# A gated mix of sliding-window attention and a SwiGLU block on one core: transposed scores that skip a place, another deal of product steps, later early tiles, and V's first quarter ordered by kind

## The chip, the cores and the metric

The kernel runs on one core of a Trainium2 chip. The metric is the device time of one execution in microseconds, and the runs of a kernel are summarised by their median. All times in this document are microseconds unless ns is written.

## The reference, cut to what matters

```python
def reference(A_x, A_wqkv, A_wo, B_x, B_w_gate, B_w_up, B_w_down, gate_w):
    x = A_x                                          # 1 x 2048 x 512
    g = _sigmoid((x * gate_w).sum(-1, keepdims=True))
    a = _A_ref(x, A_wqkv, A_wo)      # 32 heads of 16, window of 256 keys
    b = _B_ref(x, B_w_gate, B_w_up, B_w_down)   # silu(x wg) * (x wu), times wd; F = 1792
    return g * a + (1 - g) * b
```

The attention is causal within a window: query i sees keys i - 255 to i. Scores are scaled by 1/4, go through a softmax, weigh the values, and the heads are projected by `wo`. All is float32.

## The kernel before

Products that must be exact to float32 are made of three products of rounded halves: each operand is split into a rounded part (`hi`, or names that end in h) and the remainder (`lo`, or names that end in l), and hi x hi, hi x lo and lo x hi are summed in a bank of PSUM. There are eight banks, kept under the names pa, pb, pc and pd, two each, which are dealt out in turn by `bank`. The order of work on every engine is written out by hand: what stands first in the program is issued first on its queue.

**Prologue (lines 119 to 272).** x and the weights of V come by DMA in four blocks k of 128 rows of the contraction. Each block is split, the rounded part on ScalarE (ACT), the remainder on VectorE (DVE) for x and, for V's weights, on DVE for block 0 and on GpSimd (POOL) for blocks 1 to 3 (lines 173 to 178). V's first quarter (four blocks b of rows of x, in four accumulators, two to each of pa and pb) is summed k by k as the blocks come, and within a k block by block: for each b its three products (lines 214 to 217). The rest of V and the products of Q and K follow (line 381).

**The attention stage (lines 469 to 843).** Heads go in eight groups g of four. Time is counted in slots k; four slots make a step t, and sixteen steps a group. In each slot, one score of a coming group is made (`stage1`, a matmul at line 603, then a masked maximum on DVE at line 605) and one transposed score (`stage2`, a matmul at line 642, then the exponential on ACT at line 644, then selections on POOL at lines 646 and 649). Scores and transposed scores use 64 or 63 rows of the array, and each belongs to one half of the rows; two matmuls on different halves run at once. The remaining time is filled with steps of `stream`, the gate and up products of the SwiGLU block (line 564): in a step each half of the rows does one product of 512 columns, and a sum over 12 products per half is copied out by ACT (`copy_out`, line 511) in the slot where its second half ends. How many steps a slot gets is `DEAL[t >= g7][part][hd]`, with `part` the step's place among four and `hd` the slot in the step; g7 = 112 is the first step of the last group.

Every fourth step t (part 0, from t = 4 on), after the steps of slot 1, a value product is issued (`av`, line 664): 96 matmuls of 64 rows by 32 columns, each in two passes, or 64 of them where a group begins, into one bank of pc and one of pd, which `evacuate` then copies out: ACT the second bank (line 675), DVE the first (line 681; in the last group line 677 adds the two). Below, a visit is a value product with the slots up to the next. In this stage pd has two banks; transposed scores take them in turn, and the value product takes one in between. From t = 112 on, there are no scores left; transposed scores are issued two at a time in slots 0 and 2, out of three banks.

**The last group** also prepares what the next stage needs. `tile_early` makes the first two tiles of silu(gate) x up: an exponential on ACT (line 748), four operations on DVE (lines 749 to 752, the reciprocal at 750 the longest), and the split into halves, ACT first and then DVE (line 753). Each operation is hung on a slot through `at` (lines 787 to 790); the tile's inputs are loaded at slots 4 (g7 + 9) + 1 and + 2 (line 786). `prepare` splits the next weights of the stream (ACT a cast, POOL the remainder), three slots after the last sum of the ones before. After the last step, tile 2 goes through the Silu of ACT (line 760), which needs another table.

**The final stage (from line 845)** multiplies the tiles by `wd`, projects the attention's output and writes the result.

Of the kernel before, what the change touches and what calls it, by code (L numbers as in the profile page):

```python
# [12 lines left out]
ALU = mybir.AluOpType  # L13
# [5 lines left out]
NK = D // P  # L19
NB = S // P  # L20
CH = 512
NCH = S // CH
G = H // 4
NF = F // P
VW = 4 * (DH + 1) + DH
NSLOT = 4
# [7 lines left out]
def gated_mix(ctx, tc, xT, xn, wqk, wv, wo, wgu, wd, gw, out):  # L34
# [4 lines left out]
    nc = tc.nc  # L39
# [27 lines left out]
    def split(hi, lo, src, hi_eng, lo_eng):  # L67
        if hi_eng is nc.scalar:
            nc.scalar.copy(hi, src)
        else:  # L70
            hi_eng.tensor_copy(hi, src)
        lo_eng.tensor_tensor(out=lo, in0=src, in1=hi.bitcast(F32), op=ALU.subtract)
# [14 lines left out]
    def run(gen, n=None):  # L87

        while n is None or n > 0:
            if next(gen, run) is run:  # L90
                break
            n = n and n - 1
# [19 lines left out]
    def bank(n):  # L112
        names = BANKS[n if isinstance(n, str) else ("pa", "pb", "pc", "pd")[n]]
        names.append(names.pop(0))
        return psum.tile([P, CH], F32, name=names[-1])
# [7 lines left out]
    wvh = vpool.tile([P, NK, D], F32R, name="wvh")  # L123
    wvl = vpool.tile([P, NK, D], F32R, name="wvl")
# [8 lines left out]
    def u_tile():  # L133
        return wide.tile([P, CH], F32, name="u", bufs=6)
# [6 lines left out]
    def xk(c, k):  # L141
        return halves_of(xraw[2 * c + k // 2])[k % 2]

    wvraw = [u_tile() for _ in range(NK)]
# [20 lines left out]
    def fill_v(t):  # L165
        nc.gpsimd.memset(t, 0.0)
        for i in range(2):
            nc.gpsimd.memset(t[:, :, i, :68].rearrange("p g (j e) -> p g j e", e=17)[:, :, :, DH], 1.0)

    def split_x(c, k):  # L170
        split(xhi[c][:, k], xlo[c][:, k], xk(c, k), nc.scalar, nc.vector)

    for k in range(NK):
        split_x(0, k)
        split(wvh[:, k], wvl[:, k], wvraw[k], nc.scalar, nc.vector if k == 0 else nc.gpsimd)
        if k == 1:
            fill_v(vs[0])
    fill_v(vs[1])

    def v_products(b):  # L180
        c, o = divmod(b * P, CH)
        return [(xt[c][:, k, o:o + P], wt[:, k]) for k in range(NK)
                for xt, wt in ((xhi, wvh), (xhi, wvl), (xlo, wvh))]
# [24 lines left out]
    def vproj(b, ps, ks=range(NK)):  # L208
        todo = v_products(b)
        for k in ks:  # L210
            for n in range(3 * k, 3 * k + 3):
                nc.tensor.matmul(ps, *todo[n], start=n == 0, stop=n == 3 * NK - 1)

    first = [bank(n // 2) for n in range(4)]
    for k in range(NK):
        for b in range(4):
            vproj(b, first[b], (k,))
    for c in (1, 2):
# [250 lines left out]
    with ExitStack() as A:  # L469
# [14 lines left out]
        def at(k, *fs):  # L484
            AT.setdefault(k, []).extend(fs)
# [14 lines left out]
        def tick_end():  # L500
            for f in AT.pop(NOW[0], ()):
                f()
# [88 lines left out]
        def stage1(g, qb):  # L591

            hf, b = divmod(qb, NB // 2)
            if b == 0:
                MX[g, hf] = sm.tile([P, 4, NB // 2], F32, name="mx")
            q0, k0 = qb * P, max(0, qb - 2) * P
            n = q0 + P - k0
            for hd in range(4):
                pr, j = divmod(hd, 2)
                r = slice(64 * j, 64 * j + 63)  # L600

                ps = bank("pd") if g == 0 and pr else bank("pc")
                nc.tensor.matmul(ps[:, :n], QT[g % 2][pr][r, q0:q0 + P], KT[g % 2][pr][r, k0:k0 + n],  # L603
                                 start=True, stop=True)
                mx = nc.vector.tensor_tensor_reduce(out=ps[:, :n], in0=ps[:, :n], in1=mask[:, 3 * P - n:],  # L605
                                                    scale=1.0, scalar=NEG, op0=ALU.add, op1=ALU.max,
                                                    accum_out=MX[g, hf][:, hd, b:b + 1])
                if g == 0:
                    BEHIND.append(mx)
                yield  # L610
# [20 lines left out]
        def stage2(g, kb):  # L631


            n = min(3, NB - kb) * P
            k0 = kb * P
            for hd in (1, 0, 3, 2):
                pr, j = divmod(hd, 2)
                r = slice(64 * j, 64 * j + 64)
                if j:
                    pt = PT[g, kb, pr] = ptp.tile([P, 2, 3 * P], F32, name="pt")  # L640
                ps = bank("pd")
                nc.tensor.matmul(ps[:, :n], KT[g % 2][pr][r, k0:k0 + P], QT[g % 2][pr][r, k0:k0 + n],  # L642
                                 start=True, stop=True)
                BEHIND.append(nc.scalar.activation(pt[:, j, :n], ps[:, :n], AF.Exp, scale=SCALE))  # L644
                if not j:
                    nc.gpsimd.affine_select(out=pt[:, :, :P], in_=pt[:, :, :P], pattern=[[0, 2], [1, P]],  # L646
                                            compare_op=ALU.is_ge, fill=0.0, base=0, channel_multiplier=-1)
                    if n == 3 * P:
                        nc.gpsimd.affine_select(out=pt[:, :, 2 * P:], in_=pt[:, :, 2 * P:],  # L649
                                                pattern=[[0, 2], [-1, P]], compare_op=ALU.is_ge, fill=0.0,  # L650
                                                base=-1, channel_multiplier=1)
                yield
# [34 lines left out]
        first = chain(*(stage1(0, b) for b in range(NB)))  # L687
# [52 lines left out]
        def tile_load(n, place):  # L740
            GOT[n] = [h.bitcast(F32) for h in halves_of(pieces[place])]
            for i in range(2):
                nc.sync.dma_start(GOT[n][i], raws[n, i, 0])

        def tile_early(n):
            gt, up = GOT[n]
            sg, TILE[n] = kept(), halves_of(pieces[TILE_AT[n]])
            for f in (lambda: nc.scalar.activation(sg, gt, AF.Exp, scale=-1.0),
                      lambda: nc.vector.tensor_scalar(sg, sg, 1.0, None, op0=ALU.add),
                      lambda: nc.vector.reciprocal(sg, sg),  # L750
                      lambda: nc.vector.tensor_tensor(out=sg, in0=gt, in1=sg, op=ALU.mult),
                      lambda: nc.vector.tensor_tensor(out=sg, in0=up, in1=sg, op=ALU.mult),
                      lambda: split(*TILE[n], sg, nc.scalar, nc.vector)):
                f()
                yield
# [28 lines left out]
            wd_early(4 * (g7 + 1 + m) + 2, m, m)  # L784
        for n in range(2):
            at(4 * (g7 + 9) + 1 + n, lambda n=n: tile_load(n, RAW_AT[n]))
        for n, ticks in enumerate(((1, 3, 3, 3, 3, 12), (7, 9, 9, 9, 9, 19))):
            early = tile_early(n)
            for m in ticks:
                at(4 * (g7 + 10) + m, lambda early=early: run(early, 1))  # L790
# [11 lines left out]
            spread(4 * (16 * g + 9) + 3, 1, stack(g + 2, 0))  # L802
            spread(4 * (16 * g + 17) + 1, 1, stack(g + 2, 1))

        DEAL = [[[(hd + 1) * n // 4 - hd * n // 4 for hd in range(4)] for n in deal] for deal in ((5, 9, 8, 8), (8, 8, 8, 8))]
        DEAL[0][0] = 1, 2, 2, 0
        scores = chain(*(stage1(*divmod(b, NB)) for b in range(NB, G * NB)))
        run(scores, 1)
        for t in range(G * NB + 1):
            g, i = divmod(t, NB)  # L810
            d, part = divmod(t, NSLOT)
            s2 = stage2(g, i) if t < G * NB else iter(())
            values = part == 0 and t > 0
            if t == g7:
                BANKS["pc"].remove("pb1")
                BANKS["pd"].append("pb1")
            for hd in range(4):
                k = NOW[0] = NSLOT * t + hd
                run(scores, 1)
                if t < g7:  # L820
                    run(s2, 1)
                elif hd % 2 == 0:
                    run(s2, 2)
                if t == G * NB and hd == 0:
                    last_tile = tile_silu(2)
                    run(last_tile, 1)
                if t < G * NB:
                    run(steps, DEAL[t >= g7][part][hd])
                if hd == 1 and values:
                    av(*divmod(d - 1, NCH))  # L830
                    for f in LULL.pop(k, []) + UNDER:
                        f()
                    UNDER.clear()
                    evacuate(*divmod(d - 1, NCH))
                tick_end()
            if i in (7, 15) and g + 1 < G:
                UNDER.append(lambda g=g, i=i: put_max(g + 1, i // 8))
            if t >= 10 and t % 4 == 2 and t + 6 < G * NB:
                load_v((t + 6) // 4)
# [195 lines left out]
```

## Time and profile before

| | us |
|---|---|
| median of three runs (822.34 to 822.65) | 822.5 |
| the profiled execution | 822.11 |
| its span, first to last instruction | 820.4 |
| outside the span | 1.7 |

A row of a timeline reads: start, length, engine, line, operation, output <- inputs, shape, count, and in brackets the engine's idle time before it and what ended that. PE is TensorE's matmuls, PEld its weight loads, POOL GpSimd, q an engine's queue. Lengths of matmuls are modelled and overlap, so starts tell more than lengths. A row of the stages (two numbers with a colon) reads: from and to, width, busy time of PE, PEld, DVE, ACT and POOL with the count of instructions, TensorE's granted clock, the share of the DMA engines and GB/s. The granted clock is 1.00 in every row used here.

### The profile page before, as it was taken

The page shows a single profiled execution, that of the slowest core. Times are in us where ns is not written, and L with a number is a line of the kernel's source. Part 1 is how long each engine was busy: PE and PEld are TensorE (multiplying, and loading weights), DVE is VectorE, ACT ScalarE, POOL GpSimd, SP SyncE. Part 2 cuts the span into 40 slices and gives each one's busy share as a digit, 9 for nine tenths or more (in the row PEclk, how much of TensorE's full clock was granted, in tenths as well). Part 3 has the DMA queues.
Part 4 walks back from the last instruction along what each step waited for, and adds up shares of the span by engine and source line. Part 5 has one row for each costly group of instructions (what it writes and reads, how often), then busy time and mean ns, then how long its engine had stood idle before and what let it go on. Part 6 is the DMA issues. An engine that isn't in the chain of part 4 may idle for free.

```text
span 820.4 us, 20498 instructions
## 1 busy us (share of the span) xinstructions
PE 812.0 (99%) x7681; PEld 681.0 (83%) x7681; DVE 550.4 (67%) x1425; ACT 470.0 (57%) x956; POOL 402.1 (49%) x715
## 2 busy tenths in 40 slices
PE   9999999999999999999999999999999999999997
PEld 7888888878888888888888888888887888888886
DVE  5675554248877888878888887786576666554652
ACT  7455553312576767767677676776776563435340
POOL 5124442260366666767667576665873205442320
PEclk9999999999999999999999999999999999999999
DMA  8446666385625654566555655352659997878611
GB/s 302 148 156 254 231 231 235 137 268 178 218 85 194 189 179 157 182 213 202 171 167 168 207 188 159 132 170 89 212 191 349 271 287 229 273 226 221 213 52 52
DMA packets 80211, 159.70 MB, mean 195 GB/s; under 512 B 14960, under 2 KB 19440, under 8 KB 80112
## 3 DMA queue, kind: packets, MB, share of 16 engines
q1 hardware_dynamic: 68544, 127.44, 47.5%
q0 software_dynamic: 10992, 29.91, 11.3%
q8 instruction: 60, 0.98, 0.5%
q10 hardware_dynamic: 576, 1.05, 0.4%
q14 instruction: 39, 0.32, 0.1%
HBM read 93.32 MB, written 65.01 MB: 193 GB/s over the span
## 4 chain that ended last, share of the span: by engine, by line
PE 95%; DMA 2%; DVE 1%; ACT 1%; POOL 0%; SPq 0%; issue 0%; DVEq 0%; ACTq 0%
PE pa L564 22%; PE pb L564 10%; PE pd L642 6%; PE pc L664 5%; PE pd L381 4%; PE pb L381 4%; PE pa L381 4%; PE pd L81 3%; PE pc L81 3%; PE pc L83 3%; PE pd L83 3%; PE pc L82 3%; PE pd L82 3%; PE pb L664 2%; PE pc L381 2%; PE pb L83 2%
## 5 line engine op out<-in xcount | busy, mean ns | idle before, releaser
L644 ACT ACTIVATE pt<-pd 128x384 f32<-128x384 f32 (+2 forms) x491 | 223.0, 474 | 43.9 <-PE pd L642 25.6
L605 DVE CUSTOM_DVE_ANT_0 pc<-pc,mask 128x384 f32<-128x384 f32 (+2 forms) x322 | 173.2, 548 | 23.5 <-PE pc L603 9.6
L642 PE MATMUL pd<-q,k 64*128 64x384 f32 (+2 forms) x491 | 167.2, 348 | 1.8 <-ACT pt L644 1.8
L564 PE MATMUL pa<-xhi,wh 64*128 64x512 f32 x492 | 168.5, 395 | 0.0
L564 PE MATMUL pa<-xlo,wh 64*128 64x512 f32 x492 | 167.6, 394 | 0.0
L564 PE MATMUL pa<-xhi,wl 64*128 64x512 f32 x492 | 165.9, 395 | 0.0
L646 POOL TENSOR_SCALAR_AFFINE_SELECT pt<-pt 128x256 f32<-128x256 f32 x256 | 110.9, 434 | 67.9 <-ACT pt L644 62.7
L642 PEld LDWEIGHTS pd<-q,k 64*128 64x128 f32 x491 | 90.8, 185 | 26.1 <-ACT pt L644 9.8
L603 PE MATMUL pc<-k,q 63*128 63x384 f32 (+2 forms) x322 | 106.9, 337 | 0.0
L564 PE MATMUL pb<-xhi,wl 64*128 64x512 f32 x244 | 96.2, 394 | 0.0
L564 PE MATMUL pb<-xhi,wh 64*128 64x512 f32 x244 | 96.2, 394 | 0.0
L564 PE MATMUL pb<-xlo,wh 64*128 64x512 f32 x244 | 96.2, 394 | 0.0
L649 POOL TENSOR_SCALAR_AFFINE_SELECT pt<-pt 128x256 f32<-128x256 f32 x224 | 94.3, 421 | 0.0
L605 DVE CUSTOM_DVE_ANT_0 pb<-pb,mask 128x384 f32<-128x384 f32 (+2 forms) x158 | 86.9, 550 | 6.9 <-PE pb L603 3.0
L564 PEld LDWEIGHTS pa<-xhi,wh 64*128 64x128 f32 x492 | 88.2, 185 | 1.9 <-DVE mx L605 0.5
L564 PEld LDWEIGHTS pa<-xhi,wl 64*128 64x128 f32 x492 | 87.0, 185 | 1.1
L564 PEld LDWEIGHTS pa<-xlo,wh 64*128 64x128 f32 x492 | 86.9, 185 | 0.6
L605 DVE DVE_READ_ACCUMULATOR2_ANT mx<- 128x1 f32 x512 | 72.8, 142 | 0.0
L921 DVE TENSOR_TENSOR sg<-got,sg 128x512 f32<-128x512 f32 x52 | 41.1, 790 | 45.2 <-ACT sg L920 39.4
L664 PE MATMUL pd<-pt,vg 64*32 64x320 f32 (+4 forms) x1184 | 63.1, 346 | 0.0
L603 PEld LDWEIGHTS pc<-k,q 63*128 63x128 f32 x322 | 58.6, 184 | 4.8 <-issue 4.3
L682 POOL TENSOR_TENSOR oe<-oe,ob 128x512 f32<-128x512 f32 (+1 forms) x28 | 35.2, 1256 | 54.5 <-ACT ob L675 51.5
(307 smaller groups left out, 2050.8 us busy)
## 6 DMA issues: line engine op xcount, KB each, us to landing
got<-raws SPq DMA_DIRECT2D x104, 256.0 KB
raws<-ev SPq DMA_DIRECT2D x91, 256.0 KB
q<-xd SPq DMA_DIRECT2D x96, 128.0 KB
k<-xd SPq DMA_DIRECT2D x96, 128.0 KB
xd<-cx SPq DMA_DIRECT2D x16, 512.0 KB
xd<-cy SPq DMA_DIRECT2D x16, 512.0 KB
od<-oe POOLq DMA_DIRECT2D x32, 256.0 KB, 3.4
raw<-wgu SPq DMA_DIRECT2D x25, 256.0 KB
```

The source lines that it names most:

```text
L81: nc.tensor.matmul(ps, lh, rh, start=start and i == 0, stop=False, skip_group_check=skip)
L82: nc.tensor.matmul(ps, lh, rl, start=False, stop=False, skip_group_check=skip)
L83: nc.tensor.matmul(ps, ll, rh, start=False, stop=stop and i == n - 1, skip_group_check=skip)
L381: nc.tensor.matmul(ps, l[:, w], r[:, k], start=n in (1, 2, 5) and k == m == 0, stop=k == 1 and m == 2, skip_group_check=True)
L564: mm = nc.tensor.matmul(ps[o], w[r], x[r], start=first and i == 0, stop=(o is odd or bool(lane)) and i == turn - 1)
L603: nc.tensor.matmul(ps[:, :n], QT[g % 2][pr][r, q0:q0 + P], KT[g % 2][pr][r, k0:k0 + n], start=True, stop=True)
L605: mx = nc.vector.tensor_tensor_reduce(out=ps[:, :n], in0=ps[:, :n], in1=mask[:, 3 * P - n:], scale=1.0, scalar=NEG, op0=ALU.add, op1=ALU.m ...
L642: nc.tensor.matmul(ps[:, :n], KT[g % 2][pr][r, k0:k0 + P], QT[g % 2][pr][r, k0:k0 + n], start=True, stop=True)
L644: BEHIND.append(nc.scalar.activation(pt[:, j, :n], ps[:, :n], AF.Exp, scale=SCALE))
L646: nc.gpsimd.affine_select(out=pt[:, :, :P], in_=pt[:, :, :P], pattern=[[0, 2], [1, P]], compare_op=ALU.is_ge, fill=0.0, base=0, channel_mu ...
L649: nc.gpsimd.affine_select(out=pt[:, :, 2 * P:], in_=pt[:, :, 2 * P:], pattern=[[0, 2], [-1, P]], compare_op=ALU.is_ge, fill=0.0, base=-1, ...
L664: nc.tensor.matmul(AV[g, c][h][32 * j:32 * j + 32, q0 - c * CH:q1 - c * CH], VG[4 * g + kb // 4][o, kb % 4, 17 * j:17 * j + 32], PT[g, kb, ...
```

## The change

Four edits. In the prologue, block 0 of V's weights is rounded by DVE rather than ACT, ahead of the splits of x on DVE's queue; and the first quarter's products of k = 0 are issued by kind, the four blocks' hi x hi first, then the four with the weights' remainder, then the four with x's remainder. In the attention stage, the transposed scores become one chain over all steps: in slot 2 of every step with a value product none is issued, so that the chain runs one place late, and in slot 1 of part 2 two are issued, which catches up. The deal of steps for t < 112 becomes 6, 8, 8, 8 over the four parts in place of 5, 9, 8, 8, with part 0 as 1, 2, 2, 1. In the last group, tile 0's exponential moves one slot later and tile 1's split three slots later.

```diff
+    nc.vector.tensor_copy(wvh[:, 0], wvraw[0])
+    nc.vector.tensor_tensor(out=wvl[:, 0], in0=wvraw[0], in1=wvh[:, 0], op=ALU.subtract)
     for k in range(NK):
         split_x(0, k)
-        split(wvh[:, k], wvl[:, k], wvraw[k], nc.scalar, nc.vector if k == 0 else nc.gpsimd)
+        if k:
+            split(wvh[:, k], wvl[:, k], wvraw[k], nc.scalar, nc.gpsimd)
         if k == 1:
             fill_v(vs[0])
...
     first = [bank(n // 2) for n in range(4)]
-    for k in range(NK):
+    for n in range(3):
+        for b in range(4):
+            nc.tensor.matmul(first[b], *v_products(b)[n], start=n == 0, stop=False)
+    for k in range(1, NK):
         for b in range(4):
             vproj(b, first[b], (k,))
...
-        for n, ticks in enumerate(((1, 3, 3, 3, 3, 12), (7, 9, 9, 9, 9, 19))):
+        for n, ticks in enumerate(((2, 3, 3, 3, 3, 12), (7, 9, 9, 9, 9, 22))):
...
-        DEAL = [[[(hd + 1) * n // 4 - hd * n // 4 for hd in range(4)] for n in deal] for deal in ((5, 9, 8, 8), (8, 8, 8, 8))]
-        DEAL[0][0] = 1, 2, 2, 0
+        DEAL = [[[(hd + 1) * n // 4 - hd * n // 4 for hd in range(4)] for n in deal] for deal in ((6, 8, 8, 8), (8, 8, 8, 8))]
+        DEAL[0][0] = 1, 2, 2, 1
         scores = chain(*(stage1(*divmod(b, NB)) for b in range(NB, G * NB)))
+        transposed = chain(*(stage2(*divmod(b, NB)) for b in range(G * NB)))
...
-            s2 = stage2(g, i) if t < G * NB else iter(())
...
                 if t < g7:
-                    run(s2, 1)
-                elif hd % 2 == 0:
-                    run(s2, 2)
+                    run(transposed, 0 if t and (part, hd) == (0, 2) else 2 if t > NSLOT and (part, hd) == (2, 1) else 1)
+                elif t < G * NB and hd % 2 == 0:
+                    run(transposed, 2)
```

## The prediction

> **What bounds the kernel now.** The page's head and its chain come first, then the stages.
>
> ```profile
> span 820.4 us, 20498 instructions
> ...
> PE 95%; DMA 2%; DVE 1%; ACT 1%; POOL 0%; SPq 0%; issue 0%; DVEq 0%; ACTq 0%
> 226.37:568.38 342.01, 342.01 (x4854) 290.47 (x4851) 277.66 (x950) 245.05 (x545) 228.10 (x476) 1.00 0.52 168
> ```
>
> TensorE sets the end, so the change can only give time where TensorE stands or starts late. The last row (width, then busy time of PE, PEld, DVE, ACT, POOL) is the stage with value products up to the last group. Its busy PE hides stalls, since matmuls are pipelined and two run at once on the two halves of the rows. I therefore read starts. An undisturbed slot first:
>
> ```profile
> 348.32 0.34 PE L603 MATMUL pc<-k,q 63*128 63x384 f32 x1
> 348.50 0.34 PE L642 MATMUL pd<-q,k 64*128 64x384 f32 x1
> ...
> 348.97 0.34 PE L603 MATMUL pb<-k,q 63*128 63x384 f32 x1
> ```
>
> A slot with two scores and two product steps takes 0.65 here (348.32 to 348.97), and a score holds its half 0.18. Behind a value product:
>
> ```profile
> 343.99 0.34 PE L642 MATMUL pd<-q,k 64*128 64x384 f32 x1
> ...
> 344.18 0.39 PE L564 MATMUL pa<-xhi,wh 64*128 64x512 f32 x1
> 344.29 0.34 PE L603 MATMUL pc<-k,q 63*128 63x384 f32 x1
> 344.41 0.39 PE L564 MATMUL pa<-xlo,wh 64*128 64x512 f32 x1
> 344.54 0.44 PE L642 MATMUL pd<-q,k 64*128 64x384 f32 x1
> 344.65 0.40 PE L603 MATMUL pb<-k,q 63*128 63x384 f32 x1
> 344.93 0.44 PE L642 MATMUL pd<-q,k 64*128 64x384 f32 x1
> ...
> 345.50 0.33 PE L603 MATMUL pc<-k,q 63*128 63x384 f32 x1
> ...
> 346.13 0.34 PE L603 MATMUL pc<-k,q 63*128 63x384 f32 x1
> ```
>
> A product holds its half 0.23 (344.18 to 344.41). The half of the score at 344.29 has that score, one transposed score and two products before its next score at 345.50: 2 x 0.18 + 2 x 0.23 = 0.82, but 1.21 pass, 0.39 too many. The other half, from 344.65 to 346.13, holds two scores and four products: 1.28, and 1.48 pass, 0.20 too many. The mean, **0.30 lost behind a value product**, is what the first edit is about. Who is waited for (total, times, longest), and ACT there:
>
> ```profile
> PEld pd L642 <- ACT pt L644: 5.6, 28, 0.4
> PEld pd L642 <- ACT ob L675: 5.2, 26, 0.2
> ```
>
> ```profile
> 343.90 0.59 ACT L675 COPY ob<-pd 128x512 f32<-128x512 f32 x1 [1.99 <-POOL wl L72]
> 344.38 0.50 ACT L644 ACTIVATE pt<-pd 128x384 f32<-128x384 f32 x1
> ```
>
> Transposed scores have two pd banks and the value product takes one. So the score at 344.54 waits for the bank that ACT copies out from 343.90, and that at 344.93 for the exponential from 344.38 to 344.88, itself behind the copy.
>
> **The scores that skip a place.** With nothing in slot 2, the first transposed score comes in slot 3 in the free bank, the next in slot 4 in the copied one, about 0.15 after the copy is out (344.49, wanted near 344.7). The third wants the first's bank two slots on. Both waits go: 27 visits (t = 4 to 108) x 0.30 = **8.1 gained**. ACT then idles until slot 3's score; its later work covers that no more than now.
>
> Three visits have a cast of weights in that place as well:
>
> ```profile
> 281.11 0.62 ACT L69 CAST wh<-raw 128x512 fp32r<-128x512 f32 x1
> ```
>
> ```profile
> 281.85 0.33 PE L603 MATMUL pb<-k,q 63*128 63x384 f32 x1
> 282.17 0.44 PE L642 MATMUL pd<-q,k 64*128 64x384 f32 x1
> ...
> 283.37 0.34 PE L603 MATMUL pc<-k,q 63*128 63x384 f32 x1
> ```
>
> The score at 282.17 is 0.14 late (281.85 + 0.18 is 282.03). Up to its next score at 283.37 this half holds two scores and four products, 1.28, but 1.52 pass: 0.24 in all, 0.10 of it behind the wait, in the restart. With the skip the cast runs before the first exponential: 3 x 0.24 = **0.7 gained**.
>
> What it adds: at part 2, slot 1, two transposed scores stand in one slot, and the second wants the bank of the score one slot earlier on its own half: 0.18 + 2 x 0.23 + 0.18 = 0.82 later. A bank's turn (score, exponential, release) is 0.94 (343.99 to 344.93). So a **new wait** of 0.12, and behind it in PE's queue stand that slot's four products. It costs between nothing (if the other half, whose own transposed score is issued ahead of it, and the loads behind it absorb it) and 0.22 (wait plus restart as at 282.17). I take 0.10, as the other half is busy through most of it: 27 x 0.10 = **2.7 lost**.
>
> **The deal.** The count of steps stays 30 a visit, and a sum ends every 12. Counted from the loops, sums that ended in slots 4, 9, 15 of even visits now end in 3, 9, 15; 7, 12 of odd ones become 6, 12. Each end puts a copy on ACT, which holds it 0.48 (as the copy of the same shape at 343.90 does, up to 344.38). In the 13 even visits it falls between the first and the second late exponential. That one is then some 0.68 late (the two late scores come some 0.25 apart and an exponential runs 0.50, so 0.20 behind the first, then 0.48 behind the copy), and the bank's slack is 2 x 0.65 - 0.94 = 0.36: a wait of 0.32. Bounds: nothing, or 0.32 + 0.10 = 0.42; the nearest row is the cast above, of a like length between two exponentials, so 0.24: **3.1 lost**. In the 14 odd visits it lies two slots ahead of the double score and may delay its bank by up to half the copy; between 0 and 0.24 I take 0.10, near the lower end because two slots of ACT's slack lie between: **1.4 lost**. Sum of both edits: 8.8 - 7.2 = 1.6 gained. POOL's selections (228.10 busy of 342.01) and DVE (277.66) follow with room; the last scores before a value product keep their slots, so its inputs are no later.
>
> **The early tiles.** No DMA moves with them. Tile 0:
>
> ```profile
> 600.96 0.63 ACT L748 ACTIVATE ev<-k 128x512 f32<-128x512 f32 x1 [0.45 <-DMA k<-raws]
> 601.49 0.60 ACT L69 CAST wh<-raw 128x512 fp32r<-128x512 f32 x1
> ```
>
> ```profile
> 601.22 0.33 PE L642 MATMUL pb<-q,k 64*128 64x384 f32 x1
> 602.53 0.44 PE L642 MATMUL pd<-q,k 64*128 64x384 f32 x1 [0.99 <-ACT pt L644]
> ```
>
> ACT waits 0.45 for the tile's load, then runs its exponential (0.53 to the cast) before the scores' exponentials that TensorE needs. One slot later, those start 0.45 + 0.53 = 0.98 sooner, and the tile's exponential delays the next pair by up to 0.53. Between 0.45 and 0.98 I take 0.7; DVE's work on the tile hangs on the same exponential and starts 0.6 or so later, with its reciprocal off the path. Tile 1's halves:
>
> ```profile
> 615.33 0.62 ACT L69 CAST q<-ev 128x512 fp32r<-128x512 f32 x1 [1.01 <-DVE ev L752]
> ...
> 618.85 0.63 ACT L760 ACTIVATE ev<-k 128x512 f32<-128x512 f32 x1
> ```
>
> ```profile
> 615.35 0.22 PE L642 MATMUL pb<-q,k 64*128 64x128 f32 x1
> 616.18 0.32 PE L642 MATMUL pd<-q,k 64*128 64x128 f32 x1 [0.61 <-ACT pt L644]
> ```
>
> ACT stands 1.01 for DVE with the last exponentials behind it, and TensorE 0.83. Three slots later they go first. What is late next is ACT's own chain: cast, copy, table load and Silu run until 619.48 now, and the copy that frees the last value product's bank is queued behind them, so part of the 0.83 comes back there. Between 0 and 0.83 I take 0.4. Both: **1.1 gained**.
>
> **V's first quarter.**
>
> ```profile
> 10.73 1.55 POOL L72 TENSOR_TENSOR wvl<-u,wvh 128x512 fp32r<-128x512 f32 x1
> ```
>
> ```profile
> 6.72 0.62 ACT L69 CAST xhi<-q 128x512 fp32r<-128x512 f32 x1 [0.45 <-DMA q<-xT]
> ```
>
> ```profile
> L71 DVE CAST k<-ev 128x512 fp32r<-128x512 f32 x4 | 2.4, 607 | 1.0 <-DMA ev<-wd 1.0
> ```
>
> ```profile
> 7.06 0.50 PE L212 MATMUL pa<-wvl,xhi 128*128 128x512 f32 x1 [0.23 <-DVE wvl L72]
> ...
> 12.64 0.39 PE L212 MATMUL pa<-wvl,xhi 128*128 128x512 f32 x1
> ```
>
> By kind, four products run on the first weights before their remainder is needed, so the 0.23 of idling before 7.06 goes. DVE's copy (607 ns where it makes the same cast elsewhere) replaces one on ACT of 0.62, so the first weights come no later; ACT's next cast is no sooner for it, since it waits for x (6.72, idle 0.45 before). From the third block on the remainder that POOL ends at 12.28 (10.73 + 1.55) binds: its product can start near 12.33, not 12.64. So **0.3 gained**, which is also the upper bound while POOL binds; the lower is 0.
>
> **Sum.** 1.6 + 1.1 + 0.3 = 3.0 off the profiled 822.11 (its span 820.4 and 1.7 around it) is 819.1. The runs' median is 0.39 above that execution, so I forecast **819.5**.
>
> **Rivals.** *Waits absorbed:* TensorE's queue swallows the new waits; 8.8 + 1.4 = 10.2 gained, 812.3. For it: L642 waits for pt only 28 times in the stage's 342 us; against it: the 0.94 turn. 0.10.
>
> *Halves start in order:* then the double score would hold the other half's products too, 0.18 on one half, 0.09 in the mean, 27 x 0.09 = 2.4 more: 821.9, no change.
>
> ```profile
> 180.54 0.39 PE L564 MATMUL pb<-xhi,wh 64*128 64x512 f32 x1
> 180.55 0.44 PE L603 MATMUL pc<-k,q 63*128 63x384 f32 x1
> 180.78 0.39 PE L564 MATMUL pb<-xlo,wh 64*128 64x512 f32 x1
> ```
>
> Here the loop issues three products of one half before the scores, yet a score on the other half starts ahead of the second product. So 0.07. The Trainium skill ("TensorE: Matmul & The Clock Gate", Part 3, The mechanism) says that matmuls start and end strictly in program order and only weight loads are pulled ahead; by that the sum would be this rival's, and this trace disagrees (180.55 before 180.78).
>
> *The stall only moves:* new waits eat all 8.8 and the last group gives nothing but the prologue: 822.2; 0.11.
>
> *ACT binds (slower):* every new wait costs its upper bound, 27 x 0.22 + 13 x 0.42 + 14 x 0.24 = 14.8 against 8.8; with 1.4 from the rest 4.6 lost: 827.1. It decides from a mean price of 0.38 a visit on. For it: the 0.94 turn and the cast's 0.24; against: ACT is busy 245.05 of 342.01. 0.27.
>
> **How the numbers follow.** Forecast 0.45 (own range 816.5 to 820.8), absorbed 0.10, in order 0.07, moved 0.11, ACT binds 0.27, which starts at 824.2. A measurement tells 0.2%, 1.6, from no change. Faster 0.55, same 0.18, slower 0.27. The range 815.3 to 826.0 leaves out most of the first rival and the upper end of the last.
>
> **What would show it.** Right: behind value products no transposed score waits for ob, L642's waits for pt move to part 2 slot 1, and the stands of 1.31 and 0.83 in the last group shrink; TensorE's 12.64 row comes near 12.33. Wrong: waits of 0.3 and more in slots 6 and 9 of every visit.

## The result and the profile after

| | before | after |
|---|---|---|
| median of the timed runs | 822.42 us (822.07 to 822.75) | 825.67 us (825.46 to 826.73) |
| the profiled execution | 822.11, span 820.4 | 825.46, span 823.7 |

The changed kernel takes 1.0035 of the time of the one before (95% interval 1.0019 to 1.005): 3.3 us slower, where 819.5 was forecast. The time lies in the range, the sign is wrong.

The first fence is the changed kernel's page: its head and its chain by engine. The second is its view by windows for the same stage as before, from t = 4, the step of the first value product, to the first step of the last group.

```profile
span 823.7 us, 20498 instructions
...
PE 98%; DMA 1%; DVE 0%; ACT 0%; POOL 0%; issue 0%; DVEq 0%; ACTq 0%
```

```profile
core 0: us, PE busy (x) PEld busy (x) DVE busy (x) ACT busy (x) POOL busy (x), PEclk, DMA share, GB/s
226.25:571.76 345.51, 345.47 (x4855) 293.09 (x4851) 273.44 (x950) 243.46 (x545) 229.54 (x476) 1.00 0.52 167
```

The stage took 342.01 and now takes 345.51: the whole loss, 3.50, is in the visits. ACT and DVE are no busier there (243.46 and 273.44 after, 245.05 and 277.66 before), POOL by 1.4, and the clock stays full. So the loss is a wait. The view of waits for this stage says whose (total, times, longest):

```profile
PEld pd L648 <- ACT pt L650: 12.9, 60, 0.3
```

The changed file has six more lines ahead of this place, so L648 is the transposed score that was L642, L650 its exponential. The 26 waits for the copied bank (ob) are gone, as the edit meant. The waits for an exponential rose from 28 to 60, and their sum from 5.6 to 12.9. In the visit that the prediction quoted, the transposed scores behind the value product now start without a stand. The first three of them in the timeline of TensorE:

```profile
345.65 0.33 PE L648 MATMUL pd<-q,k 64*128 64x384 f32 x1
...
345.87 0.36 PE L648 MATMUL pd<-q,k 64*128 64x384 f32 x1
...
346.71 0.34 PE L648 MATMUL pd<-q,k 64*128 64x384 f32 x1
```

These take their lengths of 0.33 to 0.36; the two that waited were 0.44 long before, which is how a restart shows. Four slots on comes the place with two transposed scores, slot 9 of an even visit. TensorE there, and below it its weight loads:

```profile
348.84 0.33 PE L648 MATMUL pd<-q,k 64*128 64x384 f32 x1
...
349.30 0.35 PE L648 MATMUL pd<-q,k 64*128 64x384 f32 x1
349.48 0.34 PE L609 MATMUL pc<-k,q 63*128 63x384 f32 x1
349.75 0.44 PE L648 MATMUL pd<-q,k 64*128 64x384 f32 x1
349.76 0.67 PE L570 MATMUL pa<-xlo,wh 64*128 64x512 f32 x2
350.09 0.57 PE L570 MATMUL pa<-xhi,wl 64*128 64x512 f32 x2
350.33 0.34 PE L609 MATMUL pb<-k,q 63*128 63x384 f32 x1
350.50 0.50 PE L570 MATMUL pa<-xhi,wh 64*128 64x512 f32 x1
```

```profile
349.20 0.18 PEld L648 LDWEIGHTS pd<-q,k 64*128 64x128 f32 x1
349.25 0.18 PEld L609 LDWEIGHTS pc<-k,q 63*128 63x128 f32 x1
349.75 0.18 PEld L648 LDWEIGHTS pd<-q,k 64*128 64x128 f32 x1 [0.32 <-ACT pt L650]
349.75 0.29 PEld L570 LDWEIGHTS pa<-xlo,wh 64*128 64x128 f32 x2
```

The second score of the pair (349.75) wants the bank of the score at 348.84, 0.91 earlier: the bank's turn, as foreseen. What was not foreseen is what stands with it. The wait is on the score's weight load, and no load behind it in the queue starts before it, for either half: the other half's product load comes at 349.75 too. That other half had ended its score at 349.30 + 0.18 = 349.48, starts its product at 349.76 (0.28 lost), and its next score at 350.33, where two products of 0.23 would have ended at 350.22 (0.11, the restart): 0.39. The waiting half loses 0.09 (349.66 to 349.75) and 0.11 (349.75 + 0.18 + 0.46 is 350.39, the next product 350.50): 0.20. The mean is 0.30, to the hundredth what a value product's wait cost before (0.39 and 0.20). In all 27 visits, no product of slot 9 starts on either half before the second score of the pair.

In odd visits the bank's turn itself is longer. There a sum ends in slot 6, and ACT's copy of it (361.32) stands ahead of the exponentials of slots 7 and 8. ACT in the next visit, which is odd, then the transposed score of slot 8 and the weight load of the second score of the pair, which wants its bank:

```profile
361.32 0.59 ACT L517 COPY ev<-pa 128x512 f32<-128x512 f32 x1
361.80 0.88 ACT L650 ACTIVATE pt<-pd 128x384 f32<-128x384 f32 x2
```

```profile
361.63 0.33 PE L648 MATMUL pd<-q,k 64*128 64x384 f32 x1
```

```profile
362.73 0.18 PEld L648 LDWEIGHTS pd<-q,k 64*128 64x128 f32 x1 [0.20 <-ACT pt L650]
```

The turn is 1.10 here; by the starts in the trace it is 1.05 to 1.16 in odd visits, and 0.91 in all even ones but one (1.04). So in odd visits the loss in slot 9 is that of the pair and of the copy together, and no run here parts them.

The sum of the time lost, made as above for every slot of the 27 visits (how far each half's queue has come at its end, less 0.175 for each score and 0.228 for each product, which is how undisturbed ones follow each other, mean of both halves), gives the table below; it is worked out from all starts in the trace. Slot 2, with the value product itself, is left out.

```text
lost per visit, us, in slot     3    4    5    6    7    8    9   10   11   12   13   14   15
before, even visits           .05  .31  .02  .01  .07  .01  .00  .00  .00  .08  .01  .00  .00
after, even visits            .00  .04  .01  .21  .01  .01  .31  .11  .01  .01  .01  .00  .00
before, odd visits            .04  .29  .07  .01  .00  .00  .00  .00  .00  .01  .02  .02  .07
after, odd visits             .01  .04  .02  .01  .02  .01  .35  .01  .01  .02  .02  .03  .08
```

In the last group, the chain of waits of the changed kernel runs as follows (start, length, what). Below it stand the last value product in TensorE's timeline and POOL's timeline ahead of it:

```profile
618.62 0.83 DVE k L72
619.45 0.94 DVE den L464
620.38 0.28 issue
620.67 0.50 POOL rd L466
621.23 0.43 POOL raws L518
621.66 0.12 issue
621.78 0.43 POOL pt L652
622.25 0.32 PE pc L670 x8
```

```profile
618.57 2.22 PE L670 MATMUL pc<-pt,vg 64*32 64x320 f32 x66
622.25 0.88 PE L670 MATMUL pc<-pt,vg 64*32 64x64 f32 x30 [1.47 <-POOL pt L652]
```

```profile
620.67 0.56 POOL L466 DMA_DIRECT2D rd<-den  x1 [0.90 <-DVE den L464]
621.23 0.55 POOL L518 DMA_DIRECT2D raws<-ev  x1
621.78 0.77 POOL L652 TENSOR_SCALAR_AFFINE_SELECT pt<-pt 128x256 f32<-128x256 f32 x2
```

Both stands of 0.99 and 0.61 that the early tiles caused have shrunk, and the last value product now waits 1.47 in their stead. POOL's queue holds a DMA (rd<-den) that waits for DVE's reciprocal of the denominators (L464), and the last selections stand behind that DMA. Before, they stood so too. TensorE and POOL there:

```profile
616.84 2.68 PE L664 MATMUL pc<-pt,vg 64*32 64x320 f32 x96
```

```profile
617.06 0.56 POOL L460 DMA_DIRECT2D rd<-den  x1 [0.53 <-DVE den L458]
617.62 0.55 POOL L512 DMA_DIRECT2D raws<-ev  x1
618.17 0.77 POOL L646 TENSOR_SCALAR_AFFINE_SELECT pt<-pt 128x256 f32<-128x256 f32 x2
```

Counted from the first step of the last group (568.38 before, 571.76 after), the last selections start at 49.79 before and at 50.02 after, 0.2 later, and so does the reciprocal they stand behind (47.43 and 47.67). The value product starts at 48.46 before and at 46.81 after, 1.65 sooner. So the 1.47 is for the most part TensorE coming sooner to selections that came just in time before and have not moved with it.

### The profile page after: what moved, and what is told of

It reads as the page before. It is cut to its first block, busy times and chain, and to the rows that moved or that the text cites. A ratio compares the mean times of both kernels' runs of the same rounds, so it can differ in the third digit from the quotient of the medians.

```text
span 823.7 us, 20498 instructions
## 1 busy us (share of the span) xinstructions
PE 815.5 (99%) x7681; PEld 683.0 (83%) x7681; DVE 550.0 (67%) x1426; ACT 467.9 (57%) x955; POOL 404.3 (49%) x715
## 3 DMA queue, kind: packets, MB, share of 16 engines
q10 hardware_dynamic: 576, 1.05, 0.4%
## 4 chain that ended last, share of the span: by engine, by line
PE 98%; DMA 1%; DVE 0%; ACT 0%; POOL 0%; issue 0%; DVEq 0%; ACTq 0%
PE pa L570 23%; PE pb L570 11%; PE pd L648 6%; PE pc L670 5%; PE pd L387 4%; PE pb L387 4%; PE pa L387 4%; PE pd L81 3%; PE pc L81 3%; PE pc L83 3%; PE pd L83 3%; PE pc L82 3%; PE pd L82 3%; PE pc L609 2%; PE pb L670 2%; PE pc L387 2%
## 5 line engine op out<-in xcount | busy, mean ns | idle before, releaser
L650 ACT ACTIVATE pt<-pd 128x384 f32<-128x384 f32 (+2 forms) x491 | 219.3, 475 | 49.2 <-PE pd L648 26.3
L648 PE MATMUL pd<-q,k 64*128 64x384 f32 (+2 forms) x491 | 164.7, 348 | 0.3 <-ACT pt L650 0.2
L570 PE MATMUL pa<-xhi,wl 64*128 64x512 f32 x492 | 163.4, 391 | 0.0
L648 PEld LDWEIGHTS pd<-q,k 64*128 64x128 f32 x491 | 90.3, 184 | 24.4 <-ACT pt L650 15.4
L570 PEld LDWEIGHTS pa<-xhi,wh 64*128 64x128 f32 x492 | 86.0, 185 | 1.9 <-DVE mx L611 0.5
L570 PEld LDWEIGHTS pa<-xlo,wh 64*128 64x128 f32 x492 | 85.1, 185 | 0.5
```

The lines of the kernel that those rows point to most:

```text
L570: mm = nc.tensor.matmul(ps[o], w[r], x[r], start=first and i == 0, stop=(o is odd or bool(lane)) and i == turn - 1)
```

## The experiments

The kernel before took 823.6, 823.1, 822.8 and 823.4 in the four groups of runs that follow, each with a spread of 4 to 5 us; so ratios are given, and the stage of the visits, which the trace of each run shows to 0.1, beside them. Where the two disagree, the stage is the better guide: in the traces of `longer_both` and `parity` below, the last group, which their edits leave alone, takes 1.8 and 1.7 more than before, and why stays open.

**The parts alone.** `scores_alone` has the skip, the catching up and the deal, and nothing else of the change:

```diff
-... for deal in ((5, 9, 8, 8), (8, 8, 8, 8))]
-        DEAL[0][0] = 1, 2, 2, 0
+... for deal in ((6, 8, 8, 8), (8, 8, 8, 8))]
+        DEAL[0][0] = 1, 2, 2, 1
+        transposed = chain(*(stage2(*divmod(b, NB)) for b in range(G * NB)))
...
+                    run(transposed, 0 if t and (part, hd) == (0, 2) else 2 if t > NSLOT and (part, hd) == (2, 1) else 1)
```

> The kernel before with the skipped place and the deal 6, 8, 8, 8 alone. Theory (the visits carry the slowdown: the wait behind the value product goes, but slot 9, where two transposed scores stand, loses 0.3 to 0.4 in each of 27 visits, and slot 6 another 0.2 in the 13 even ones): 3.0 to 4.0 slower than before. Rival (the visits break even, and the last group's work on DVE, which holds up the last value product, carries the slowdown): within 0.7 of before.

Measured: 825.53, ratio 1.0032 (1.0018 to 1.0047). Its stage of visits lasts 344.71, against 342.01 before, and its slots lose what the change's do (0.31 and 0.36 in slot 9, 0.22 in slot 6 of even visits). The scores and the deal carry the slowdown. It is a little smaller than expected: 2.7 in the stage, 2.6 by the ratio. Of the 3.5 in the changed kernel's trace, 0.8 is not here; 0.3 of that lies in a single visit, and the rest is not explained.

`tiles_alone` has both early tiles later, `tile1_alone` the halves of tile 1 only:

```diff
-        for n, ticks in enumerate(((1, 3, 3, 3, 3, 12), (7, 9, 9, 9, 9, 19))):
+        for n, ticks in enumerate(((2, 3, 3, 3, 3, 12), (7, 9, 9, 9, 9, 22))):
```

> The kernel before with the early tiles' two moves alone. Theory (the stands of 1.31 and 0.83 shrink, but tile 0's reciprocal starts later on DVE and pushes the second tile, the inversion of the shares and a DMA on POOL, behind which the last selections wait, so the last value product stands): between 0.5 faster and 0.8 slower, with the last value product waiting over 1 us for POOL. Rival (the last group carries the slowdown): 2.5 to 3.5 slower. The prediction's own term: 1.1 faster.

> The kernel before with tile 1's split three slots later alone, tile 0 as it was. Theory (the harm comes from tile 0's later start on DVE): 0.4 to 0.8 faster, and no wait over 0.5 us of the last value product for POOL. Rival (moving the split is what delays the shares' inversion or runs into the table load): within 0.2 of before or slower.

Measured: 822.92, ratio 0.9989 (0.9975 to 1.0003), and 822.6, ratio 0.999 (0.9976 to 1.0003): neither can be told from no change. Their timelines show the last value product, of `tiles_alone` first, then of `tile1_alone`:

```profile
618.90 0.88 PE L664 MATMUL pc<-pt,vg 64*32 64x64 f32 x30 [1.47 <-POOL pt L646]
```

```profile
618.85 0.88 PE L664 MATMUL pc<-pt,vg 64*32 64x64 f32 x30 [0.50 <-POOL pt L646]
```

Tile 1's halves give TensorE 0.8 back just ahead of the value product, which then starts 0.6 sooner, waits 0.50 and ends no sooner than before: POOL's last selections come when they came. So less came than was expected of `tile1_alone`. With tile 0 later as well, the value product starts another 1.0 sooner (615.24 for 616.22), POOL's selections stand within 0.2 of where they stood, and it waits 1.47. So it is not a push of tile 0 on DVE's chain, as the expectation had it, that makes the wait.

What tile 0's move gives hangs on when the tile's load lands. With its exponential in the old slot, ACT waited 0.45 to 0.65 for that load in three traces (the kernel before, `scores_alone`, `tile1_alone`), and 12.88 to 13.05 passed from the value product of t = 120 to the next; in five traces (`v_alone`, `parity` and the three `longer` ones below) it did not wait, and 12.28 to 12.31 passed. In the six traces with the exponential moved it is 12.10 to 12.13. So the move gives some 0.8 where the load is late, and 0.2 where it is not.

`v_alone` has V's first quarter by kind, with its first weights rounded on DVE as in the change:

```diff
-    for k in range(NK):
+    for n in range(3):
+        for b in range(4):
+            nc.tensor.matmul(first[b], *v_products(b)[n], start=n == 0, stop=False)
+    for k in range(1, NK):
```

> The kernel before with V's first quarter by kind alone. Theory (POOL's remainders bind, and each wait for them costs a restart): 0.1 faster, the attention stage starting 0.1 sooner in the trace. Rival (the prediction's term): 0.3 faster.

Measured: 824.06, ratio 1.0003 (0.9989 to 1.0018). In its trace the products of Q and K start 0.27 earlier, counted from the first product; a gain of this size a timed run here does not tell from nothing.

**What makes the double dear.** If it is the bank's turn with the queue behind it, the loss must move with the spacing of the scores. `longer_ahead` is `scores_alone` with one line more; `longer_both` has 3, 3, 1, 1 in that line; `longer_copies` has 3, 3, 2, 1 there and the deal 5, 8, 9, 8 with 1, 2, 1, 1 in its first part:

```diff
+        DEAL[0][2] = 3, 1, 2, 2
```

> As scores_alone (825.5), but the slot ahead of the two transposed scores (part 2, slot 0) gets three product steps and the slot with the two gets one (3, 1, 2, 2 in place of 2, 2, 2, 2). Theory, the bank's turn: a transposed score needs the bank of the one before the last, and that is free 0.94 us after that one started. Ahead of the second score of slot 9 the spacing grows from 0.91 to about 1.1, so slot 9's standing of 0.30 to 0.38 falls to 0.1 or less; but the score in slot 10 then comes only some 0.7 after the first of slot 9, so about 0.25 of it comes back in slot 10. In all 0 to 3 us below scores_alone, the place of the wait moved by one slot. Rival, the order of the halves (three scores in a slot, two of them on one half, leave the other half idle whatever the banks do): slot 9 keeps its 0.3, and the time that of scores_alone within 0.5.

> As scores_alone, but part 2 deals 3, 3, 1, 1: the slot ahead of the two transposed scores and the slot with them both have three product steps. Theory, the bank's turn: all three spacings around the double are then 0.94 or more (about 1.1, 1.0, 1.2), so slots 9 and 10 stand 0.1 or less together and slot 12 some 0.1: of the 0.30 to 0.38 some 0.2 a visit comes back, 27 x 0.2 = 5.4 us below scores_alone, 819 to 822. Rival, the order of the halves: slot 9 keeps 0.3, time within 1 of scores_alone.

> As longer_both, but with the deal 5, 8, 9, 8 (first part 1, 2, 1, 1, third part 3, 3, 2, 1), so that the sums end, and ACT's copies stand, in the slots that they have in the kernel before (4, 9, 15 and 7, 12). Theory: the 0.20 to 0.24 that even visits stand in slot 6 is the copy between the two late exponentials and goes with it: 13 x 0.2 = 2.6 us below longer_both. Rival: those 0.2 belong to the late exponentials themselves (two transposed scores after the value product's banks come back), and stay: within 0.5 of longer_both.

| | time | ratio | stage of visits | where the slots lose |
|---|---|---|---|---|
| scores_alone | 825.53 | 1.0032 | 344.71 | 9: .31/.36 (even/odd), 10: .10/.01, 6: .22/.01 |
| longer_ahead | 831.33 | 1.0099 (1.0082 to 1.0115) | 349.60 | 9: .04/.08, 10: .60/.41, 6: .22/.01 |
| longer_both | 828.41 | 1.0062 (1.0044 to 1.008) | 347.26 | 9: .10/.12, 10: .05/.01, 12: .44/.21, 6: .22/.01 |
| longer_copies | 826.26 | 1.0037 (1.0024 to 1.0051) | 345.51 | 9: .11/.30, 12: .18/.02, 4: .19/.20, 6: .01/.01 |

The place of the loss followed the spacing: slot 9 fell to 0.04 to 0.12 as soon as the slots around it were longer. The one exception is the odd visits of `longer_copies` (0.30), where a sum ends in slot 7: ACT's copy of it delays the exponential of slot 8, and the second score of the pair starts 1.24 behind that slot's score, against 1.05 in even visits. The rival (two scores on one half cost by themselves) is out. But the sizes were missed each time: what left slot 9 came back at the next short slot, and more of it than expected. `longer_ahead`'s waits for its stage and one of them in its weight loads:

```profile
PEld pd L642 <- ACT pt L644: 17.2, 42, 0.6
```

```profile
352.44 0.18 PEld L642 LDWEIGHTS pd<-q,k 64*128 64x128 f32 x1 [0.64 <-ACT pt L644]
```

Fewer waits than in `scores_alone` (61), but twice as long. Where they come back in `longer_both` tells more: in slot 12, and most in even visits, where a sum ends in slot 9 and ACT copies it out in between (0.44, against 0.21 in odd visits). And `longer_copies`, whose sums end where they ended before, lost nothing in slot 6: that 0.22 is the copy between the two late exponentials, as the prediction had it. (`parity` below shows it more cleanly: there slots 2 to 6 of even visits are dealt as in the change, the sum ends in slot 4 in place of 3, and slot 6 loses nothing.) It paid in slot 4 instead, because slots 2 and 3 with one step each let the second late score come before the value product's bank is copied.

`parity` put the double into slot 13 of even and slot 10 of odd visits, away from the copies, with even visits of 31 steps and odd ones of 29 (the last of 30). Its skip and its two lines of dealing:

```diff
+                    run(transposed, 0 if t and (part, hd) == (0, 2) else 2 if t > NSLOT and (part, hd) == ((2, 2) if d % 2 else (3, 1)) else 1)
...
+        EVEN = (1, 2, 2, 1), (2, 2, 2, 3), (2, 2, 2, 1), (3, 3, 1, 2)
+        ODD = (1, 2, 2, 1), (2, 2, 2, 1), (2, 3, 3, 1), (2, 2, 1, 2)
```

> The transposed scores skip their place behind the value product as in the change, but the two that share a slot stand where no copy of a sum is near: slot 13 of even visits, slot 10 of odd ones, with three product steps in that slot and in the one ahead; and even visits deal 31 steps, odd ones 29, so that the first copy of an even visit stays in slot 4. Theory, the queue behind the bank's turn: a wait for a bank holds up all weight loads behind it, so it costs both halves; the double costs little only where both its spacings exceed 0.94 and ACT has no copy within two slots. Slots 3 and 4 stay at 0.05 together, slot 6 of even visits falls from 0.22 to below 0.05, the slot of the double to 0.15 or less: 27 x (0.35 - 0.20) + 13 x 0.05 = 4 to 5 us below the kernel before, 817.5 to 820 where that is 822.5. Rival, ACT has no room for the extra exponential anywhere in a visit: the stall moves once more and the time is within 1.5 of the kernel before or above it.

Measured: 827.36, ratio 1.0047 (1.0029 to 1.0066), stage 345.48: a miss. Slot 6 was clear and the doubles cost 0.09 and 0.07 in their own slots, but slot 12 of even visits lost 0.28 and slots 9 and 15 of odd ones 0.21 and 0.27. Each of these comes three slots after the one in which a sum ends, and one of the two slots before it has one step only. The exponential behind the copy is late, which lengthens one bank's turn from 0.94 to as much as 0.94 + 0.48 = 1.42 (the score that waits starts 1.40 behind the one whose bank it wants in slot 12, and 1.23 in slots 9 and 15, in the median). Two slots of two steps last 1.28; with one of the two at one step, (2 x 0.18 + 2 x 0.23) / 2 = 0.41, they last 1.05. By this the deal, not the double, made these; `clear` below puts it to the test.

**The queue on POOL.** `rd_later` is `tiles_alone` with the DMA of the reciprocals behind the last selections:

```diff
-            for n in (0, 8, 11):
+            for n in (0, 8, 16 if c else 11):
```

> As tiles_alone (both early tiles later, 822.9), with one more edit: the DMA that puts the last group's reciprocals away (rd<-den, on POOL's queue ahead of the last selections) is issued five slots later, behind them. Theory: the last value product waits 1.47 for POOL's selection only because that DMA stands in POOL's queue until DVE has made the reciprocals, which the later tiles delay; with it behind the selections the wait goes and the gain of both stands in d30 and d31 is kept: 1.2 to 1.7 us below tiles_alone, 821.2 to 821.7. Rival: the selections are late by their own exponentials, and the time is that of tiles_alone within 0.3.

Measured: 821.18, ratio 0.9978 (0.9967 to 0.9988), faster than before. Its last value product runs through, without a wait, and ends with 618.33 (row below), where the one of `tiles_alone` ended at 619.78:

```profile
615.50 2.83 PE L664 MATMUL pc<-pt,vg 64*32 64x320 f32 x96
```

So the theory holds: that DMA's place in the queue decides whether the early tiles gain anything. In this execution DVE's reciprocal also came 1.0 sooner than in the changed kernel; but in the traces of `all_rd` and `clear`, which have the same edit, it comes when it came there (47.7 after the start of the last group), and their last value product runs through without a wait as well (that of `rest_rd` waits 0.40). `rest_rd` adds V by kind to it, and `all_rd` adds `parity` to that:

> The change without its scores and deal: V's first quarter by kind, both early tiles later, and the reciprocals' DMA behind the last selections. Theory: rd_later's gain plus the 0.1 to 0.3 of the prologue: ratio to before 0.997 to 0.998, some 820.5 to 821.2. Rival: the prologue gives nothing or less: ratio 0.998 or above.

> parity and rest_rd together. Theory: the parts stand in different stages and add: the gain of parity plus that of rest_rd, 815 to 818.5 by the first theory of parity; by its rival 820 to 822.

Measured: 821.44, ratio 0.9982 (0.9972 to 0.9992), and 824.57, ratio 1.0018 (1.0009 to 1.0028). V by kind adds nothing that shows. The second lies above both times that were expected of it; the parts add up within their intervals, with `parity`'s loss.

**A deal that leaves room behind the copies.** `clear` is `rd_later` with the skip and the double of `parity`, 30 steps in each visit and no slot of one step within two slots behind a copy (but for slot 0, which had one step before too):

```diff
+        EVEN = (1, 2, 2, 1), (3, 2, 1, 2), (1, 2, 2, 2), (3, 3, 1, 2)
+        ODD = (1, 2, 2, 1), (2, 1, 2, 2), (2, 3, 3, 1), (2, 2, 2, 2)
```

> rd_later's last group with the skip once more, dealt so that no slot of one product step stands within two slots behind a copy of a sum (30 steps in each visit; even 1221 3212 1222 3312 with the double in slot 13, odd 1221 2122 2331 2222 with the double in slot 10). Theory, the queue behind the bank's turn: in parity the stalls stood where a short slot followed a copy (slot 12 of even visits 0.28, slots 9 and 15 of odd ones 0.21 and 0.27); here each pair of slots behind a copy lasts 1.28 or more and the double's spacings 0.94 or more, so these fall to 0.15 a visit together and the visits gain 27 x 0.15, 4 us: 816.5 to 818.5 where the kernel before is at 822.5, 3 below rd_later. Rival, the extra exponential has no room in any place: the visits stay within 1 of the kernel before's, and the time at rd_later's 821 or above.

Measured: 817.3, ratio 0.9925 (0.9907 to 0.9943), as expected. The stage by windows and its waits:

```profile
226.74:564.92 338.18, 338.12 (x4854) 286.97 (x4851) 267.31 (x950) 240.66 (x545) 228.57 (x476) 1.00 0.53 170
```

```profile
PEld pd L642 <- ACT pt L644: 3.7, 14, 0.4
```

The visits take 3.8 less than before and 7.3 less than in the changed kernel, with the same matmuls; the doubles cost 0.06 (slot 13) and 0.02 (slot 10), and the largest loss left is 0.13, in slot 9 of even visits. So the skip is worth its price where the deal gives the banks their time. `rd_later` and `rest_rd` beat the kernel before by 0.2%, this version by 0.75%: it is the fastest of all.

## Why the prediction was wrong, point by point

**The skip: right in mechanism and size.** Slots 3 to 5 lost 8.8 less over the 27 visits (4.1 in the even, 4.7 in the odd ones, by the table's sums before rounding); 8.1 + 0.7 had been forecast. No score waits for ob.

**The double: the step that failed.** The text took 0.10 a visit, "as the other half is busy through most of it", with an upper bound of 0.22, together 2.7. Slot 9 lost 0.31 and 0.35, 8.9 in all: above the bound, and as much as the skip gave. In odd visits a copy has a share in this that is not known; in even ones the double stands alone. The wait and its cause were right; what was wrong is that the other half works on. It has only the weights that were loaded ahead of the waiting load, and here that was nothing but a score that ended at 349.48. The rows of before had shown this price already: two waits of 0.2 behind each value product cost 0.39 on one half and 0.20 on the other, while the text priced a wait of 0.12 as if one half alone had it. The wait itself was also longer, 0.32 of the load queue's time, since loads run ahead of their matmuls (349.25 for 349.48) and so reach the wait sooner.

**The copies: right in place, mis-sized.** Even visits lose 2.7 in slot 6, which the text placed there (3.1), and 1.4 more in slot 10, behind the double; but the old copies' losses in slots 7 and 12 (0.07 and 0.08, 1.7 in all) went, which the sum left out. The odd visits' copy was priced at 1.4. It does delay the double's bank there (1.10 for 0.91), and its share in the 0.35 of slot 9 is not known; slot 9 of odd visits loses 0.04 more than that of even ones, 0.6. The edits of the visits come to 8.8 - 8.9 - 1.0 (slots 6, 7 and 12 of even visits) - 1.5 (slot 10) - 0.8 (all others) = 3.4 lost, of the 3.5 that the windows show, where 1.6 gained was forecast.

**The early tiles: the hidden term.** The stands on ACT gave what was forecast or more: from one value product to the next, 0.75 in the visit of t = 120 (0.7 forecast) and 0.83 in that of t = 124 (0.4). That the first came out so near is in part luck, for it hung on a late load (0.2 where the load is in time, as above). The step that failed is "what is late next is ACT's own chain". Next was POOL: the last value product needs POOL's last selections, these stand behind a DMA in POOL's queue, and that DMA waits for DVE's reciprocal of the denominators. This chain was there before, just in time, and has no term in the sum. So the value product started 1.65 sooner and took 1.89 longer (from its start to the next product 4.50, 2.61 before). The last group as a whole moved by 0.2, lost, with 1.1 gained forecast; `rd_later` shows the gain was there. "With its reciprocal off the path" was right: DVE stood idle for 2.10 ahead of its work for the second tile before, and from the start of the last group the second tile's reciprocal comes at 41.98 before and 42.04 after.

**V's first quarter.** 0.3 was forecast, 0.17 came in the changed kernel (the attention stage starts 0.11 sooner though the first product was 0.06 later). The first product on POOL's remainder of the third block stands at 12.43 in its timeline, where 12.33 was read (POOL itself started 0.15 later, at 10.88 for 10.73), and the next at 12.75, so a restart took part of it:

```profile
12.43 0.48 PE L215 MATMUL pa<-wvl,xhi 128*128 128x512 f32 x1
12.75 0.39 PE L215 MATMUL pa<-wvh,xlo 128*128 128x512 f32 x1
```

**The rivals.** "ACT binds" came nearest in time (827.1): the double alone cost more than its upper bound, and the sign for "wrong", waits of 0.3 and more in slots 6 and 9, came in slot 9 alone (0.31 and 0.35 lost). Its condition, a mean price of 0.38 a visit, was met: slots 6 to 12 cost 0.45 more a visit. Its name was off, for ACT is no busier; banks and the load queue bind. "Halves start in order" did not show: in the rows above, matmuls of the halves start as each is free until a wait stands ahead of both (the score at 349.48 is issued ahead of the transposed one at 349.30, on the other half). "Waits absorbed" is out.

## What to carry to other kernels

Price a wait on TensorE's queue by the rows of such a wait, on both halves: everything issued behind it stands, however free its own half is, and the cover is only what was loaded before. When an order is changed to take one wait away, write down the spacing of every use of a bank around the new order, with the copies that lengthen its turn; a skip, a catching up and a deal are one edit, and here the same skip made the visits 2.7 longer or 3.8 shorter, by the place of the double and the deal. When a stand is taken away, look at what the engine needs next and at everything queued ahead of that, the DMAs on the other engine's queue among them: what came just in time before is the next wait.

## What the runs showed of the hardware

A weight load that waits for its bank holds up the loads of the other half of the rows: 0.32 of waiting cost 0.39 on the half that had nothing to wait for, 0.20 on the one that waited. The Trainium skill ("TensorE: Matmul & The Clock Gate", Part 1, Architectural detail) calls TensorE's queue a partial reorder window, which can pull weight loads ahead of matmuls in flight, and the others strict queues. The trace agrees for TensorE and POOL, within a limit: loads ran 0.23 ahead of their matmul (349.25 for 349.48), but none ran past one that waited for its bank (349.75 and 349.75); and POOL's selection stood behind a DMA that waited 0.90.

After this wait the first matmul behind is longer in the records (0.44 for 0.33 at 349.75), and 0.11 more is lost on each half.
